# Low halves of w1 moved to ScalarE and GpSimd in the ramp, the first softmax cut in two, and one visit moved up a list

## The chip, the cores and the metric

The kernel runs on one core of a Trainium2 chip. The metric is the device time of one execution in microseconds (us); the median of three runs is compared. The engines are called as the profile calls them: PE (TensorE matmul) with PEld (its weight load), DVE (VectorE), ACT (ScalarE), POOL (GpSimd), and SP (SyncE, which here issues DMAs). Each engine executes its instructions in the order of its own queue. A DMA that is issued from SP's queue waits there for its data, and everything behind it waits too.

## The reference

Two stages follow each other, in float32:

- A causal convolution with weights of its own for each token: for 8 sequences of 2880 tokens with 192 channels, `weight_gen` gives 8 heads x 7 taps for each token. A softmax over the 7 taps (maximum subtracted, exponential, divided by the sum plus 1e-9) makes the weights, and `out[b,s,h*24:(h+1)*24] = sum over k of w[b,s,h,k] * x[b,s-6+k,h*24:(h+1)*24]`, with zeros ahead of a sequence.
- A routed mixture of experts on the 23040 results: the best of 4 groups by `x @ w_group`, then the best of its 4 experts by `x @ w_expert[g]`, so one of 16 experts for each token. The token's output is `gate * (relu(x @ w1[g,e]) @ w2[g,e])`, with w1 of 192x1024 and w2 of 1024x192. The gate is the product of the two softmax values.

## The kernel before, in words

**Tiling.** The 23040 tokens lie as 128 partitions x 180 columns, and 15 groups of 12 columns are worked through in order (`front`, line 612). A group's convolution (`conv`, 284) has two chunks of 6 columns. For each tap DVE multiplies the chunk's inputs by the weights (`product`, L289, 128x1152). In the first six chunks the products are summed on PE, by a matmul with the identity into PSUM (L330); `SUMS` says which taps DVE adds by itself beforehand (L325). The products lie in a ring of three buffers, `pr`. ACT then copies the sums out of PSUM (L333). Later chunks are added on DVE alone (L307).

**Routing.** `logits` (359) takes a chunk: ACT copies the last 64 channels aside (`rem`, L379), PE transposes the rows (L386, L387), ACT copies the transposes (L393), PE multiplies by the router's weights (L369, L410), ACT copies the logits (`ls`, L413). `ranks` (417) is a row of some 30 small DVE instructions from L341 to L480; the last one writes `posi`, the position of every token in a table `rows` in HBM that is sorted by expert. Then POOL sends the group's 12 columns there, one indirect DMA each (`scatter_row`, L494).

**Visits.** After certain groups a list is made (`table`, 508) of full blocks of 128, 256 or 384 rows of one expert; `ROUNDS` says after how many groups, and how many visits of 3, 2 and 1 blocks each list holds. A visit loads its rows (`xb`, L750, on SP) and its expert's weights, does the two matmuls (L878, L916) and scatters the result (L933, on POOL). The first list comes after two groups and holds ten visits of one block, which multiply in plain float32. In the later visits w1 and x are split into a high part, rounded to `float32r`, and a low part. What is left of w1's last 64 rows after the rounding, the low half, is made once at the start for all 16 experts by `halves` (580), two experts at a time, and stored in HBM as `w1lo`; later visits read it.

**Ramp.** The stretch up to the first visit is called the ramp here: groups 0 and 1 through convolution, routing and scattering.

**Order.** The instructions of PE, ACT, DVE and SP are issued in the order in which the Python code emits them; POOL's order is chosen by the framework's scheduler. The code is a set of generators that yield what an instruction costs by the kernel's own table, and `clk` is the planner's clock for each engine, the sum of these costs. It sets the order and measures nothing. `front` steps through `conv`; after each of its yields `beside` (622) lets side work move: `slow` (the halves), `side` (the next group's softmax), and `routing`. A generator that yields `NEXT` is not moved again until `state["unit"]` has changed, and that goes up with each finished sum of products.

**The halves before.** `next(slow[0][0])` issues the 16 loads at the start. From group 2 on (`g >= FIRST`, line 624) each call of `beside` moves one step: ACT casts a pair to its high part (L591, into one shared buffer `hi`), then DVE subtracts (L593) and SP stores two results (L595).

Of the kernel before, what the change touches and what calls it, by code (L numbers as in the profile page):

```python
# [1 line left out]

# [6 lines left out]
F32 = mybir.dt.float32  # L9
F32R = mybir.dt.float32r  # L10
# [3 lines left out]
ALU = mybir.AluOpType  # L14
# [2 lines left out]
DRAM = bass.MemoryType.DRAM  # L17

WIDTHS = (12,) * 15
ROUNDS = ((2, 0, 0, 10), (3, 0, 4, 0), (4, 0, 5, 0), (5, 0, 7, 0), (6, 0, 5, 0), (7, 0, 7, 0), (8, 0, 5, 0), (9, 0, 6, 0), (10, 0, 7, 0), (11, 0, 5, 0), (12, 1, 4, 0), (13, 0, 5, 0), (14, 0, 6, 0), (15, 10, 6, 2))  # L20
LATE = (1.0, 3.0, 3.0)
AHEAD = (1.0, 1.0, 2.5)
HURRY = 12
# [1 line left out]
WHOLE = 12  # L25
SINGLE = tuple((k,) for k in range(7))
MIXED = ((0, 1), (2,), (3,), (4,), (5,), (6,))
FOUR = ((0, 1, 2), (3, 4), (5, 6))
FIVE = ((0, 1), (2, 3), (4,), (5,), (6,))
HALF = ((0, 1), (2, 3), (4, 5), (6,))  # L30
SUMS = (MIXED, FIVE, FIVE, FIVE, FIVE, FIVE)


class Slot:
# [4 lines left out]
def conv_moe_kernel(ctx: ExitStack, tc: tile.TileContext, x, wgen, w_group, w_expert, w1, w2, out):  # L39
    nc = tc.nc  # L40
    B, SEQ, D = x.shape
    H, K = wgen.shape[2], wgen.shape[3]
    G, EG = w1.shape[0], w1.shape[1]
    F = w1.shape[3]
    P = 128
    HG = D // H
    NE = G * EG
# [4 lines left out]
    SG = 12  # L52
    SC = 6
# [11 lines left out]
    MAXB = NTOK // BK  # L65
    NR = len(ROUNDS)
    ENDS = [r[0] for r in ROUNDS]
    COL = [sum(WIDTHS[:g]) for g in range(len(WIDTHS) + 1)]
# [5 lines left out]
    FIRST = ENDS[0]  # L74
    MAIN = next(r[0] for r in ROUNDS if r[1] or r[2])
    kinds = ((3, 1), (2, 2), (1, 3))

    sure = 0
    for r in ROUNDS[:-1]:
        for nb, c in kinds:  # L80
            sure = max(sure, min(sure + nb * UB * r[c], COL[r[0]] * P - NE * (nb * UB - 1)))
    left = (NTOK - sure + NE * (BK - 1)) // BK
    TAIL = max(0, -(-(left - ROUNDS[-1][2]) // TB))

# [3 lines left out]
    pool = lambda name, bufs=1, **kw: ctx.enter_context(tc.tile_pool(name=name, bufs=bufs, **kw))  # L88
# [5 lines left out]
    wp = pool("wp")  # L94
# [14 lines left out]
    grp = {}  # L109
# [88 lines left out]
    def ring(name, n, shape, dt=F32):  # L198
        tiles = [const.tile(shape, dt, name=f"{name}{i}") for i in range(n)]
        at = [0]  # L200

        def take(i=None):
            at[0] += 1
            return tiles[(at[0] if i is None else i) % n]
        return take
# [17 lines left out]
    new_raw = [ring(f"raw{i}", m, [P, n]) for i, (n, m) in enumerate(((F, 2), (F, 2), (NFT * D, 1)))]  # L223
# [11 lines left out]
    clk = {"pe": 0.0, "act": 0.0, "dve": 3.0, "pool": 0.0}  # L235
    HOP = 0.15

    def run(eng, cost, *deps):
        clk[eng] = max([clk[eng]] + [d + HOP for d in deps]) + cost
        return clk[eng]  # L240
# [8 lines left out]
    NEXT = object()  # L249
# [3 lines left out]

    TINY = 0.2

    def softmax(g):
        wt, n = grp[g].wt, WIDTHS[g] * H
        cost = 0.08 + 0.7 * WIDTHS[g] / SG
        m = cv.tile([P, SG * H, 1], F32, name="m", bufs=1)[:, 0:n, :]
        nc.vector.tensor_reduce(out=m, in_=wt, axis=AX.X, op=ALU.max)  # L260
        yield cost
        nc.vector.tensor_tensor(out=wt, in0=wt, in1=m.broadcast_to([P, n, K]), op=ALU.subtract)
        nc.scalar.activation(out=wt, in_=wt, func=AF.Exp)
        texp = run("act", cost, clk["dve"] + cost)
        yield cost
        yield Until(texp + LATE[0])
        z = cv.tile([P, SG * H, 1], F32, name="z", bufs=1)[:, 0:n, :]
        nc.vector.tensor_reduce(out=z, in_=wt, axis=AX.X, op=ALU.add)
        yield cost
        nc.vector.tensor_scalar(out=z, in0=z, scalar1=1e-9, scalar2=None, op0=ALU.add)  # L270
        yield TINY
        nc.vector.reciprocal(out=z, in_=z)
        yield 0.08 + 0.6 * WIDTHS[g] / SG
        nc.vector.tensor_tensor(out=wt, in0=wt, in1=z.broadcast_to([P, n, K]), op=ALU.mult)
        yield cost

# [3 lines left out]
    def sum_banks(k):  # L280
        at = [(3 * k + i) % 4 for i in range(3)] if k < CHUNK[FIRST] else [2, 0, 1]
        return [banks[a]([P, 2, D]) for a in at]

    def conv(g, o):
# [3 lines left out]
        def product(c0, k, dst):  # L288
            nc.vector.tensor_tensor(  # L289
                out=dst, in0=o.xin[:, c0 + k:c0 + k + SC, :].rearrange("p s (h g) -> p s h g", g=HG),  # L290
                in1=w4[:, c0:c0 + SC, :, k:k + 1].broadcast_to([P, SC, H, HG]), op=ALU.mult)

        for n, c0 in enumerate(range(0, WIDTHS[g], SC)):
            row = o.xrow[n]
            acc = row[:, :, 0:D].rearrange("p s (h g) -> p s h g", g=HG)
            new = lambda: cv.tile([P, SC, H, HG], F32, name="pr", bufs=3)
            if state["slots"] or CHUNK[g] + n >= len(SUMS):
                product(c0, 0, acc)
# [13 lines left out]
            pieces = sum_banks(CHUNK[g] + n)  # L312
            pattern = SUMS[CHUNK[g] + n]
            for j, ks in enumerate(pattern):
# [193 lines left out]
    def table(r):  # L508
# [13 lines left out]
        yield 0.6  # L522
        todo = [(nb, c) for nb, c in ((kinds[0], kinds[2], kinds[1]) if last else kinds) if ROUNDS[r][c] or last and nb == 2]
        for nb, c in todo:
# [55 lines left out]
    def halves():  # L580
        spare = wp.tile([P, 3, F], F32, name="wa", bufs=3)
        raws = [spare[:, k, :] for k in range(3)]
        raws.append(wp.tile([P, NFT, D], F32, name="wc", bufs=4).rearrange("p f d -> p (f d)")[:, 0:F])
        raws += [new_raw[k]() for k in range(2) for _ in range(2)]
        hi = new_raw[2]()[:, 0:F].bitcast(F32R)
        for raw, e in zip(raws, range(0, NE, 2)):
            for h in range(2):
                nc.sync.dma_start(out=raw[h * HP:(h + 1) * HP, :], in_=w1v[e + h, P:D, :])
        yield NEXT
        for raw, e in zip(raws, range(0, NE, 2)):  # L590
            nc.scalar.copy(out=hi, in_=raw)  # L591
            yield Until(run("act", 0.95))
            nc.vector.tensor_tensor(out=raw.bitcast(F32R), in0=raw, in1=hi.bitcast(F32), op=ALU.subtract)  # L593
            for h in range(2):
                nc.sync.dma_start(out=w1lo[e + h], in_=raw[h * HP:(h + 1) * HP, :])  # L595
            yield 1.13

    def set_up():
        nc.gpsimd.memset(tri, 1.0)
# [8 lines left out]

    scoring, ranking = [], []
    slow = [[halves(), None]]  # L610

    def front():
        side = []
        set_up()
        load_group(1)
        next(slow[0][0])
        yield from softmax(0)

        def pace(g):
            return 99 if g <= FIRST else HURRY if g < MAIN + 3 else 8 if g in ENDS else 2  # L620

        def beside(g, n):
            rush = g >= FIRST and not grp[FIRST - 1].routed
            if g >= FIRST and not rush:
                for q in list(slow):
                    yield from move(slow, q, 1)
            for q in side[:1]:
                if not rush:
                    yield from move(side, q, 3)
            yield from routing(g)  # L630

        def routing(g):
            if ranking:
                yield from move(ranking, ranking[0], pace(g))
            if scoring and (not ranking or g < FIRST):
                yield from move(scoring, scoring[0], pace(g) if scoring[0][2].chunks == 2 or g >= FIRST - 1 else 3)

        def settle(g):
            while not grp[g].routed:
                qs = ranking or scoring  # L640
                q = qs[0]
                yield from move(qs, q, 99)
                if qs and qs[0] is q and q[1] is not None:
                    yield Until(q[1][1]) if q[1][0] == "time" else NEXT

        for g in range(ENDS[-1]):
            o = grp[g]
            o.routed = False
            scoring.append([logits(g, o), None, o])
            for n, c in enumerate(conv(g, o)):  # L650
                yield c
                if n == (2 if state["slots"] else 0) and 1 <= g < ENDS[-1] - 1:
                    load_group(g + 1)
                if n >= (12 if state["slots"] else 4) and not o.ahead and g + 1 < ENDS[-1] and g != FIRST - 1:
                    o.ahead = True
                    side.append([softmax(g + 1), None])
                yield from beside(g, n)
                if g == FIRST - 1 and n in (7, 8):
                    if n == 7:
                        soft = softmax(FIRST)  # L660
                    yield next(soft)
            if g == FIRST - 1:
                for n, c in enumerate(soft):
                    yield c
                    yield from beside(g, n)
            yield from finish_all(side)
            if g:
                yield from settle(g - 1)
        yield from settle(ENDS[-1] - 1)
# [8 lines left out]
    def move(qs, q, most):  # L678
        for _ in range(most):
# [15 lines left out]
            else:  # L695
                yield c

    fr = front()

    def step():  # L700
# [446 lines left out]
```

## Time and profile before

| | us |
|---|---|
| median of 3 runs | 1255.02 |
| lowest, highest | 1247.34, 1255.09 |
| the profiled execution | 1256.81 |
| its span | 1255.2 |
| PE, DVE, ACT, POOL busy in it | 1162.0, 968.2, 651.6, 557.4 |

The page gives busy times and a chain that ended last. For a change in the ramp the timeline says more: it lists one engine's instructions in order of time, and in brackets the idle time before one and what ended it. A busy time of small instructions in a row can overlap a little, since each is counted from its issue to its end.

### The profile page before, as it was taken

What the parts mean: (1) busy time and instruction counts of PE and PEld (TensorE: products, weight loads), DVE (VectorE), ACT (ScalarE), POOL (GpSimd) and SP (SyncE); (2) the same over time, 40 slices, a digit from 0 to 9 for tenths busy, and PEclk for the clock granted to TensorE, in tenths of its full rate; (3) what the DMA queues carried; (4) which work ended last, traced back from release to release, by engine and by line L of the source; (5) the groups of instructions that cost most, each with busy time, mean ns of one, the idle gap of its engine ahead of it and who ended that gap; (6) DMA issues with size and microseconds to landing.
All of it is one profiled execution on the core that took longest, in us unless ns stands there. A gap on an engine that the chain in (4) does not pass through costs nothing.

```text
span 1255.2 us, 24437 instructions
## 1 busy us (share of the span) xinstructions
PE 1162.0 (93%) x8357; PEld 1087.6 (87%) x8357; DVE 968.2 (77%) x1648; ACT 651.6 (52%) x1234; POOL 557.4 (44%) x598
## 2 busy tenths in 40 slices
PE   5886996979999999999999999997999989999995
PEld 2443886879999999999999999997899989999995
DVE  8897895968989999999998988886554756666560
ACT  1122443536556655566555655544556656666561
POOL 6133171635547465746573737372656212222121
PEclk9897898979999999999999999998899989999998
DMA  9228789966877887978786878637678775555661
GB/s 264 92 101 253 233 263 288 255 203 196 276 235 260 249 267 233 289 217 284 214 299 204 285 224 292 192 105 247 183 230 234 235 205 150 153 157 156 182 191 37
DMA packets 81734, 270.89 MB, mean 216 GB/s; under 512 B 15063, under 2 KB 31734, under 8 KB 79808
## 3 DMA queue, kind: packets, MB, share of 16 engines
q1 hardware_dynamic: 62424, 229.77, 60.1%
q0 software_dynamic: 19056, 39.20, 9.5%
q8 instruction: 67, 1.10, 0.4%
q14 instruction: 67, 0.55, 0.2%
q10 hardware_dynamic: 120, 0.28, 0.1%
HBM read 225.83 MB, written 44.23 MB: 215 GB/s over the span
## 4 chain that ended last, share of the span: by engine, by line
PE 56%; issue 20%; DMA 7%; POOL 7%; DVE 6%; ACT 2%; SPq 1%; POOLq 0%; ACTq 0%; DVEq 0%
PE py L916 24%; PE ph L878 23%; POOL out L933 4%; DVE pr L289 2%; POOL rows L494 2%; DMA xb<-rows 2%; PE pl L369 2%; PE tp L386 1%; DMA raw<-in_moe_w 1%; DMA raw<-w1lo 1%; PE tpx L853 1%; PE tpx L852 1%; DMA wa<-in_moe_w 1%; PE ph L330 1%; PE tp L387 1%
## 5 line engine op out<-in xcount | busy, mean ns | idle before, releaser
L878 PE MATMUL ph<-xh,wa 128*128 128x256 f32 (+1 forms) x1992 | 468.2, 309 | 0.0
L933 POOL DMA_INDIRECT out<-y,xb x189 | 212.9, 1126 | 485.6 <-ACT y L925 215.0
L916 PE MATMUL py<-wc,hh 128*128 128x192 f32 x2160 | 404.1, 329 | 5.6 <-ACT y L925 5.6
L878 PE MATMUL ph<-xl,wa 128*128 128x256 f32 (+1 forms) x1328 | 360.5, 290 | 0.0
L916 PEld LDWEIGHTS py<-wc,hh 128*128 128x128 f32 x2160 | 349.6, 192 | 5.8 <-ACT y L925 5.8
L878 PEld LDWEIGHTS ph<-xh,wa 128*128 128x128 f32 x1992 | 338.9, 191 | 7.0 <-issue 5.6
L884 ACT ACTIVATE hh<-ph 128x512 f32<-128x512 f32 (+2 forms) x296 | 165.6, 560 | 271.2 <-PE ph L878 271.2
L878 PEld LDWEIGHTS ph<-xl,wa 128*128 128x128 f32 x1328 | 252.1, 190 | 0.0
L289 DVE TENSOR_TENSOR pr<-xin,wt 128x1152 f32<-128x1152 f32 x186 | 248.8, 1350 | 4.0 <-PE py L330 1.9
L494 POOL DMA_INDIRECT rows<-xrow,ix x156 | 215.3, 1380 | 52.3 <-POOL ix L493 33.0
L307 DVE TENSOR_TENSOR xrow<-xrow,pr 128x1152 f32<-128x1152 f32 x144 | 194.7, 1352 | 0.6
L811 DVE SCALAR_TENSOR_TENSOR pr<-ph,hh 128x384 fp32r<-128x384 f32 (+1 forms) x128 | 77.5, 605 | 105.0 <-ACT hh L889 103.8
L811 DVE TENSOR_TENSOR wa<-raw,wa 128x1024 fp32r<-128x1024 f32 x83 | 101.3, 1220 | 40.2 <-ACT wa L787 40.2
L918 PE MATMUL py<-wc,hh 128*128 128x384 f32 x352 | 112.8, 367 | 0.0
L493 POOL COPY ix<-posi 128x1 int32<-128x1 int32 x156 | 70.7, 463 | 80.5 <-DMA rows<-xrow,ix 44.6
L889 ACT ACTIVATE hh<-ph 128x384 fp32r<-128x384 f32 (+1 forms) x128 | 68.6, 536 | 69.6 <-PE ph L878 69.5
L787 ACT CAST wa<-raw 128x1024 fp32r<-128x1024 f32 x83 | 87.1, 1049 | 7.6 <-DMA raw<-in_moe_w 7.6
L919 PE MATMUL py<-wc,pr 128*128 128x192 f32 x352 | 89.0, 253 | 0.0
L796 ACT CAST wa<-raw 128x1024 fp32r<-128x1024 f32 x83 | 86.8, 1046 | 1.1 <-DMA raw<-w1lo 1.1
L811 DVE TENSOR_TENSOR xl<-tpx,xh 128x512 fp32r<-128x512 f32 (+1 forms) x94 | 61.6, 655 | 28.3 <-ACT xh L858 27.1
L925 ACT ACTIVATE y<-py,xb 128x192 f32<-128x192 f32 x179 | 67.4, 424 | 23.1 <-PE py L916 21.6
L393 ACT COPY xT<-tp 128x384 f32<-128x384 f32 x84 | 40.4, 481 | 62.4 <-PE pl L369 33.6
(172 smaller groups left out, 1392.5 us busy)
## 6 DMA issues: line engine op xcount, KB each, us to landing
wc<-in_moe_w SPq DMA_DIRECT2D x73, 768.0 KB, 5.5
raw<-in_moe_w SPq DMA_DIRECT2D x83, 512.0 KB, 5.2
xin<-in_x SPq DMA_DIRECT2D x14, 1728.0 KB, 10.0
raw<-in_moe_w SPq DMA_DIRECT2D x91, 256.0 KB, 5.0
raw<-w1lo SPq DMA_DIRECT2D x83, 256.0 KB, 6.5
raw<-in_moe_w SPq DMA_DIRECT2D x22, 768.0 KB, 7.8
xb<-rows SPq DMA_DIRECT2D x72, 194.0 KB, 4.4
wa<-in_moe_w SPq DMA_DIRECT2D x24, 384.0 KB, 5.8
```

The lines of the kernel that those rows point to most:

```text
L289: nc.vector.tensor_tensor(out=dst, in0=o.xin[:, c0 + k:c0 + k + SC, :].rearrange("p s (h g) -> p s h g", g=HG), in1=w4[:, c0:c0 + SC, :, k ...
L307: nc.vector.tensor_tensor(out=acc, in0=acc, in1=prs[k - 2], op=ALU.add)
L494: written_once(nc.gpsimd.indirect_dma_start(out=rows[:, :], out_offset=bass.IndirectOffsetOnAxis(ap=ix, axis=0), in_=src, in_offset=None, ...
L787: nc.scalar.copy(out=o.wa[:, 0, :], in_=o.raw[0])
L796: nc.scalar.copy(out=o.wa[:, 2, :], in_=o.raw[1])
L811: f(*a, **k)
L878: nc.tensor.matmul(ph[:, v, :], lhsT=w[:, f0:f0 + P], rhs=rhs, start=i == 0, stop=i == len(terms) - 1)
L884: nc.scalar.activation(out=hh, in_=ph, func=AF.Relu)
L916: nc.tensor.matmul(b.acc[t], lhsT=hh[:, v, c], rhs=wc[0][:, f, :], start=f == 0 and not (b.wide and t == 1), stop=f == NFT - 1 and not (b. ...
L918: nc.tensor.matmul(b.py[t], lhsT=hh[:, v, c], rhs=wc[f // 4][:, f % 4].rearrange("p l d -> p (l d)"), start=f == 0, stop=False)
L919: nc.tensor.matmul(b.acc[t], lhsT=hl[:, v, c], rhs=wc[f // 4][:, f % 4, 0, :], start=False, stop=f == NFT - 1)
L933: ins = nc.gpsimd.indirect_dma_start(out=out[:, :], out_offset=bass.IndirectOffsetOnAxis(ap=b.x.bitcast(I32)[:, t, D + 1:D + 2], axis=0), ...
```

## The change

Four edits.

1. `halves` no longer uses DVE. ACT casts a pair into one of two buffers in turn (`his`, in a tile of the ring `wa`), POOL subtracts, SP stores, all emitted in one step. The steps start when the planner's clock of DVE is past 44, in whatever group, where they started with group 2.
2. The first group's softmax is done for its first six columns ahead of the convolution. The six instructions for the other six columns are emitted one after each of the first six yields of the convolution.
3. The first chunk takes its taps from the last to the first, and the two that DVE adds are 6 and 5 (before: 0 and 1).
4. The tenth list holds six visits of two blocks instead of five, the eleventh three instead of four.

```diff
-ROUNDS = (... (11, 0, 5, 0), (12, 1, 4, 0), ...)
+ROUNDS = (... (11, 0, 6, 0), (12, 1, 3, 0), ...)
...
+TURNED = ((6, 5), (4,), (3,), (2,), (1,), (0,))
-SUMS = (MIXED, FIVE, FIVE, FIVE, FIVE, FIVE)
+SUMS = (TURNED, FIVE, FIVE, FIVE, FIVE, FIVE)
...
-    def softmax(g):
-        wt, n = grp[g].wt, WIDTHS[g] * H
-        cost = 0.08 + 0.7 * WIDTHS[g] / SG
+    def softmax(g, a=0, b=None):
+        b = b or WIDTHS[g]
+        wt, n = grp[g].wt[:, a * H:b * H, :], (b - a) * H
+        cost = 0.08 + 0.7 * (b - a) / SG
...
-        hi = new_raw[2]()[:, 0:F].bitcast(F32R)
+        other = wp.tile([P, 3, F], F32, name="wa", bufs=3)
+        his = [other[:, k, :].bitcast(F32R) for k in range(2)]
...
-        for raw, e in zip(raws, range(0, NE, 2)):
+        for k, raw in enumerate(raws):
+            e, hi = 2 * k, his[k % 2]
             nc.scalar.copy(out=hi, in_=raw)
-            yield Until(run("act", 0.95))
-            nc.vector.tensor_tensor(out=raw.bitcast(F32R), in0=raw, in1=hi.bitcast(F32), op=ALU.subtract)
+            nc.gpsimd.tensor_tensor(out=raw, in0=raw, in1=hi.bitcast(F32), op=ALU.subtract)
+            run("pool", 2.0, run("act", 1.0))
             for h in range(2):
                 nc.sync.dma_start(out=w1lo[e + h], in_=raw[h * HP:(h + 1) * HP, :])
-            yield 1.13
+            yield NEXT
...
-        yield from softmax(0)
+        yield from softmax(0, 0, SC)
+        rest = softmax(0, SC)
...
-            if g >= FIRST and not rush:
+            if clk["dve"] > 44 and not rush:
                 for q in list(slow):
                     yield from move(slow, q, 1)
...
                 yield c
+                if g == 0 and n < 6:
+                    for c in islice(rest, None if n == 5 else 1):
+                        yield c
```

## Rows read from the trace of the kernel before

**Rows 1.** The page's slices: PE's busy tenths in 40 slices of the span.
```profile
PE   5886996979999999999999999997999989999995
```

**Rows 2.** Timeline: end of the ramp; start, duration, engine, line, operation, tiles.
```profile
99.93 13.95 SPq L595 DMA_DIRECT2D w1lo<-wa  x6
...
107.69 0.97 POOL L494 DMA_INDIRECT rows<-xrow,posi  x1 [0.30 <-issue]
...
115.57 1.97 SPq L750 DMA_DIRECT2D xb<-rows  x2
...
117.63 0.63 PE L843 MATMUL tp<-ident,xb 128*96 128x128 f32 x2 [3.76 <-DMA xb<-rows]
```

**Rows 3.** Tile view of `rows`: how long its DMAs took to land.
```profile
DMA to landing us min/median/max: 2.4/5.0/9.0
```

**Rows 4.** Timeline: the first softmax and the first chunk.
```profile
4.38 1.28 ACT L263 ACT_TABLE_LOAD   x1 [4.38 <-DMA wt<-in_weight_gen]
...
6.60 0.85 DVE L268 TENSOR_REDUCE z<-wt 128x96 f32<-128x672 f32 x1 [0.83 <-ACT wt L263]
...
9.51 2.65 DVE L289 TENSOR_TENSOR pr<-xin,wt 128x1152 f32<-128x1152 f32 x2
...
13.69 1.62 PE L330 MATMUL ph<-pr,ident 128*128 128x384 f32 x2 [13.69 <-POOL first L161]
```

**Rows 5.** Timeline: group 0's logits and ranks.
```profile
46.68 0.36 ACT L413 COPY ls<-pl 128x240 f32<-128x240 f32 x1 [0.64 <-PE pl L410]
...
48.35 0.49 DVE L426 TENSOR_TENSOR sel<-ls,ohg 128x192 f32<-128x192 f32 x1
...
49.73 0.21 DVE L349 SCALAR_TENSOR_TENSOR dfe<-de,j 128x48 f32<-128x48 f32 x1
...
55.74 0.17 DVE L480 SCALAR_TENSOR_TENSOR posi<-pos 128x12 int32<-128x12 f32 x1
```

**Rows 6.** Timeline: the first and the last of group 0's twelve scatters on POOL.
```profile
56.80 2.09 POOL L494 DMA_INDIRECT rows<-xrow,posi  x1 [34.96 <-DVE wt L262]
...
74.12 0.97 POOL L494 DMA_INDIRECT rows<-xrow,posi  x1 [0.30 <-issue]
```

**Rows 7.** Timeline: group 1, from its first chunk's logits to its ranks.
```profile
64.31 0.51 ACT L379 COPY rem<-xrow 128x384 f32<-128x384 f32 x1
...
66.82 0.91 PE L330 MATMUL py<-pr,ident 128*128 128x384 f32 x2
...
69.06 3.90 DVE L289 TENSOR_TENSOR pr<-xin,wt 128x1152 f32<-128x1152 f32 x3 [0.52 <-PE ph L330]
...
83.75 0.19 DVE L341 TENSOR_REDUCE mxg<-ls 128x12 f32<-128x48 f32 x1
```

**Rows 8.** Timeline: POOL beside DVE, at the start and later.
```profile
3.85 0.73 POOL L159 TENSOR_SCALAR first<-sgn 128x16 f32<-128x16 f32 x3
...
9.79 3.86 POOL L161 TENSOR_SCALAR first<-first 128x16 f32<-128x16 f32 x3
...
230.30 2.74 DVE L307 TENSOR_TENSOR xrow<-xrow,pr 128x1152 f32<-128x1152 f32 x2
...
231.72 1.37 POOL L493 COPY ix<-posi 128x1 int32<-128x1 int32 x1 [4.75 <-DMA rows<-xrow,ix]
```

**Rows 9.** Timeline: POOL's largest elementwise instruction, and one cast of the halves on ACT.
```profile
0.91 1.06 POOL L119 MEMSET xin<- 128x1152 f32 x1 [0.29 <-POOLq L1130]
...
101.89 1.05 ACT L591 CAST raw<-wa 128x1024 fp32r<-128x1024 f32 x1
```

**Rows 10.** Timeline: after the first visit's start, up to the idle time behind list one.
```profile
122.18 1.23 DVE L593 TENSOR_TENSOR wc<-wc,raw 128x1024 fp32r<-128x1024 f32 x1 [6.90 <-ACT raw L591]
...
136.33 0.36 ACT L413 COPY ls<-pl 128x240 f32<-128x240 f32 x1 [0.99 <-PE pl L410]
...
140.53 0.19 DVE L341 TENSOR_REDUCE mxg<-ls 128x12 f32<-128x48 f32 x1
...
209.44 1.65 PE L916 MATMUL py<-wc,hh 128*128 128x192 f32 x4 [5.60 <-ACT y L925]
```

More of the change, by code (lines that the diff above doesn't have):

```diff
@@ L1 @@
 from contextlib import ExitStack
+from itertools import islice
 import concourse.bass as bass
@@ L19 @@
 WIDTHS = (12,) * 15
-ROUNDS = ((2, 0, 0, 10), (3, 0, 4, 0), (4, 0, 5, 0), (5, 0, 7, 0), (6, 0, 5, 0), (7, 0, 7, 0), (8, 0, 5, 0), (9, 0, 6, 0), (10, 0, 7, 0), (11, 0, 5, 0), (12, 1, 4, 0), (13, 0, 5, 0), (14, 0, 6, 0), (15, 10, 6, 2))
+ROUNDS = ((2, 0, 0, 10), (3, 0, 4, 0), (4, 0, 5, 0), (5, 0, 7, 0), (6, 0, 5, 0), (7, 0, 7, 0), (8, 0, 5, 0), (9, 0, 6, 0), (10, 0, 7, 0), (11, 0, 6, 0), (12, 1, 3, 0), (13, 0, 5, 0), (14, 0, 6, 0), (15, 10, 6, 2))
 LATE = (1.0, 3.0, 3.0)
@@ L272, in softmax @@
         nc.vector.reciprocal(out=z, in_=z)
-        yield 0.08 + 0.6 * WIDTHS[g] / SG
+        yield 0.08 + 0.6 * (b - a) / SG
         nc.vector.tensor_tensor(out=wt, in0=wt, in1=z.broadcast_to([P, n, K]), op=ALU.mult)
```

## The prediction

> **What bounds the kernel now.** I read the page's slices first. From the tenth slice (282 us) on, PE stands at nine tenths or more in nearly all of them [rows 1], so a microsecond won or lost before that is mostly kept to the end. The low digits lie in the first nine slices, and all that the change moves lies there too, but for one visit. So the ramp is read next, as a timeline. It ends with the first visit's transposes at 117.63, released by its rows [rows 2]. Group 1's last scatter left POOL at 108.66. The load of the rows was issued only at 115.57, because SP stood at the stores of the halves for 13.95 us, waiting for DVE's subtractions. Two things therefore bound the ramp: the path convolution, logits, ranks, scatter of groups 0 and 1, and behind it SP's queue. After the first visit the next loss that a list explains is PE's 5.60 us ahead of 209.44 [rows 10].
>
> **Edit 2 and 3, the first softmax and the taps.** The sums of its first six columns start once ACT's table is loaded (5.66, rows 4) and an exponential of half the length is done: the 0.94 us up to 6.60 become some 0.5. From there to the first product are 2.9 us of DVE, half of that now. The first product starts near 7.7, 1.8 us sooner. The other six columns cost DVE half of 4.6 us (the 2.9, and two instructions like the 0.85 us reduction) and a little for more starts: 2.4 us, placed among the first products. PE's first sum needs two products and an addition and now has two of these pieces among them (0.9 us): it starts 0.9 us sooner than 13.69. At the end of the chunk the balance is between -0.9 (PE carries it through) and +0.6 (2.4 less 1.8). I take 0, in the middle. Taps from the last let the first product do without the six columns that come from the neighbour; in the rows DVE waits for no such load, so this alone is priced at 0, and its cover is that the loads landed before 9.51.
>
> **Edit 1, where the pairs stand.** The order follows from the code. The planner's clock passes 44 after the first addition of group 1's first chunk (44.9 when its costs are summed; this is an order, not a time). One pair is emitted for each new unit: pair 1 there, pair 2 after the next tap, pair 3 just ahead of group 0's ranks. Then come the ranks and POOL's twelve scatters. Pairs 4 and 5 follow behind them, pair 6 behind ACT's copies of that chunk's sums and **ahead of `rem`**, pairs 7 and 8 in the next chunk. Casts alternate between two buffers, so the cast of pair 6 waits until POOL has subtracted pair 4.
>
> *Price of a subtraction on POOL.* No row shows one. DVE takes 1.23 us for it [rows 10]. POOL's largest elementwise row, a fill of 1152 columns, takes 1.06 [rows 9], so 0.94 for 1024. The subtraction reads two tensors: at one pass 0.94, at two 1.9, at three (two reads, a write) 2.8. I take 1.9, one pass for each input. The Trainium skill ("GPSIMD Engine Reference", section "3.1 Elementwise") gives 4497 ns for such an instruction of 2048 columns, by which I estimate 2.25 us here, and the sum would be 1.4 us higher; no run here shows it yet.
>
> *DVE and POOL.* Three small POOL instructions take 0.73 us together at 3.85, beside a reduction, and 3.86 us at 9.79, beside products that read two tensors: 1.29 each, a product's length [rows 8]. At 231.72 a copy of one column lasts 1.37 us under two additions, and these last 2.74 where two products of the same size take 2.65 [rows 4, 8]. So POOL waits for such a DVE instruction to end, and DVE, as far as a tiny copy can show it, waits for POOL in turn. I take it that a subtraction on POOL stops DVE's two-tensor instructions for its length. The Trainium skill ("SBUF — State Buffer", section "SBUF: two separate sides") states this as a lock on the ports that the two share, held for the whole instruction by whoever came first. By that rule the cost below stands; without it the forecast is the rival "side by side". It speaks against this edit, and the trace agrees on POOL's side.
>
> *Group 0's ranks.* ACT is free after `ls` (47.04), the first cast ends at 48.1, and the first subtraction starts near 48.3, when DVE comes to the instruction at 48.35 [rows 5]. DVE gets one two-tensor instruction in after each subtraction: 48.3 + 1.9, then 0.5, then 1.9, then 0.2, then 1.9, is 54.7 for the instruction that stood at 49.73: **+5.0**. Ends: 0 without the exclusion, +7.7 at 2.8 us each.
>
> *The wait ahead of `rem`.* `posi` then ends at 60.9 instead of 55.91, and the twelve scatters, back to back from 56.80 to 75.09 [rows 6], end at 80.1. Only then comes pair 4's subtraction (0.3 us between POOL's instructions, 1.9) until 82.3, pair 6's cast (1.05 and a hop of 0.1) until 83.45, and `rem`, which stood at 64.31 [rows 7]: **+19.1**. Queued behind that cast on ACT are `rem` and the copies of the transposes; PE waits for these with the next chunk's sums (66.82) behind them, and DVE stops when the three product buffers are full. The excess over the 5.0 is the new wait, 14.1 us. Ends: 0 (pair 4 goes ahead of the scatters), or 14.1 less or more 0.9, by the price of the subtraction.
>
> *From there to group 1's `posi`.* Subtractions 5 and 6 fall into DVE's stop. 7 and 8 may stop DVE among the last products (0 to 3.8 us); DVE has run ahead into the products that stood at 69.06, which gives some back. I set both at 0. So group 1's ranks, at 83.75 before, and its scatters are 19.1 late.
>
> *SP and DVE at the ramp's end.* The stores now wait for POOL, and are done with pair 8, well before group 1's scatters end. Behind them in SP's queue stands only group 3's load, needed 20 us later. A scatter takes 2.4 to 5.0 us to land [rows 3], so the rows can be loaded 2.4 to 5.0 after the last one leaves POOL, where it was 6.9: 1.9 to 4.5 less. I take **-3.2**, the middle. The low end is 0: DVE loses three subtractions there, and the planner, which books none of them, puts as many products ahead of the first visit.
>
> *After the first visit.* DVE no longer subtracts, nor waits for ACT's cast (6.90 us ahead of one at 122.18). Group 2's logits were copied at 136.69, and DVE came to them at 140.53, 3.8 us later; one more subtraction of 1.2 lies between that and the list. **-5.0**, if the list is that much sooner and the 5.60 us of PE shrink with it [rows 10]. Ends: 0 and -5.6.
>
> **Edit 4.** The tenth and eleventh list hold 12 visits together before and after, and PE's slices there (22 to 27 of 40) are all 9; the 7 behind them lies at the twelfth list [rows 1]. No wait stands at the head of the eleventh: 0.
>
> **Sum.** 0 + 5.0 + 14.1 - 3.2 - 5.0 = +10.9. The profiled execution (1256.8) would become 1267.7. It lies 1.8 above the median of the runs (1255.0), so I forecast a median of **1265.9**, 0.9% slower.
>
> **The rivals.**
> - *No wait ahead of `rem`* (faster): POOL's order is the scheduler's. If it sends pair 4 ahead of the scatters, and the engines run side by side, the ramp's path is as before, and -3.2 and -5.0 remain: 1246.8. Decided by whether the fourth subtraction has ended by 62, when `rem` could start. For it: POOL idles up to 56.80. Against it: the twelve scatters are ready together and were emitted first, and nothing came between them before [rows 6].
> - *Side by side* (POOL's subtractions don't stop DVE, but the wait stands): 14.1 - 8.2 = +5.9, 1260.9. For it: DVE's loss under POOL is shown for a tiny copy only.
> - *Exclusion without the wait*: eight subtractions of 1.9 are 15.2 us of DVE in the ramp, less the 0.5 it idled there [rows 7], less 8.2: +6.5, 1261.5.
>
> **How the numbers follow.** The forecast has a chance of 0.50, no wait 0.22, side by side 0.15, exclusion alone 0.08; 0.05 is left for what I don't see. The forecast's own range is 1258 (cheap subtractions, both credits whole) to 1275 (2.8 us each, half of the credits). To hold 8 in 10 the range takes in "no wait" at 1246.8: 1246 to 1275. A measurement of this kernel tells about 1% (12.6 us) from no change. The forecast lies 1.7 us within that bound, so some two fifths of it count as slower, and most of the two middle rivals as the same; "no wait" reaches -12.6 only if both credits are at their ends and the first softmax gains too. Slower 0.30, same 0.61, faster 0.09.
>
> **What would show it.** Right: in the new trace ACT idles between the copies at L333 of group 1's first chunk and `rem`, released by POOL; the fourth subtraction starts behind twelve scatters; `rem` is at 80 to 86; group 0's `posi` is near 61; the load of the first rows follows the last scatter by less than 5 us; PE's gap near 209 is smaller. Wrong: subtractions 4 to 8 end before 70, `rem` near 64, DVE's products of usual spacing beside POOL's subtractions, or a POOL subtraction outside 0.9 to 2.8 us.

## The result, and the profile after

| | kernel before | changed kernel |
|---|---|---|
| first comparison, 12 runs each: median us | 1250.79 | 1257.26 |
| ratio, 95% interval | | 1.0056 [1.0038, 1.0074] |
| second comparison, another chip: median us | 1258.22 | 1269.38 |
| ratio, 95% interval | | 1.0093 [1.0057, 1.0128] |
| profiled execution (first comparison), span | 1256.81, 1255.2 | 1261.24, 1259.6 |

The changed kernel is slower, by 0.4 to 1.3%. The forecast was 1265.9, 0.9% (10.9 us) slower. The first comparison's difference of 6.5 us lies 4 us under that, the second's of 11.2 on it. The first median itself lies 8.6 us under 1265.9; 4.2 of these come from the kernel before, whose median was 1255.02 in the three runs that the forecast started from and is 1250.79 in twelve. The ramp went much as forecast; two later terms were wrong by some 10 us or more each, and they have opposite signs.

The page's slices of the changed kernel, PE's busy tenths and the granted clock in 40 slices of 31 us (before: [rows 1]):

```profile
PE   5657898899999999999999999969999989999995
PEclk9877899899999999999999999979999989999998
```

Of the first five slices three are lower and one is higher, the sixth to ninth are together a little higher, and the 7 at the 28th slice has become a 6 at the 27th: a stall far from the ramp has moved and grown.

The timeline of the changed kernel, several engines in order of time (line numbers are 3 to 9 higher than before; to be read beside [rows 4], [rows 5], [rows 6], [rows 7] and [rows 2]):

```profile
7.85 1.36 DVE L292 TENSOR_TENSOR pr<-xin,wt 128x1152 f32<-128x1152 f32 x1
...
47.63 0.36 ACT L416 COPY ls<-pl 128x240 f32<-128x240 f32 x1 [0.64 <-PE pl L413]
...
49.02 7.08 POOL L597 TENSOR_TENSOR wa<-wa 128x1024 f32<-128x1024 f32 x3 [27.35 <-ACT wa L596]
49.06 2.37 DVE L358 TENSOR_TENSOR ohg<-dfg,ixg 128x48 f32<-128x48 f32 x1
51.46 2.47 DVE L429 TENSOR_TENSOR sel<-ls,ohg 128x192 f32<-128x192 f32 x1
...
62.20 0.17 DVE L483 SCALAR_TENSOR_TENSOR posi<-pos 128x12 int32<-128x12 f32 x1
62.67 1.44 POOL L497 DMA_INDIRECT rows<-xrow,posi  x1 [6.58 <-DVE posi L483]
...
78.72 0.98 POOL L497 DMA_INDIRECT rows<-xrow,posi  x1 [0.30 <-issue]
79.70 2.37 POOL L597 TENSOR_TENSOR wc<-wc,wa 128x1024 f32<-128x1024 f32 x1
82.11 1.05 ACT L596 CAST wa<-raw 128x1024 fp32r<-128x1024 f32 x1 [12.99 <-POOL wc L597]
83.06 0.51 ACT L382 COPY rem<-xrow 128x384 f32<-128x384 f32 x1
88.17 5.79 POOL L597 TENSOR_TENSOR raw<-raw,wa 128x1024 f32<-128x1024 f32 x2 [1.48 <-ACT wa L596]
88.95 6.22 DVE L292 TENSOR_TENSOR pr<-xin,wt 128x1152 f32<-128x1152 f32 x2 [13.96 <-PE ph L333]
...
113.80 0.17 DVE L483 SCALAR_TENSOR_TENSOR posi<-pos 128x12 int32<-128x12 f32 x1
...
130.02 0.98 POOL L497 DMA_INDIRECT rows<-xrow,posi  x1 [0.30 <-issue]
132.66 1.47 SPq L759 DMA_DIRECT2D xb<-rows  x2
...
217.25 1.65 PE L925 MATMUL py<-wc,hh 128*128 128x192 f32 x4 [3.19 <-ACT y L934]
```

Two lines of the kernel before stand against these:

```profile
48.11 0.21 DVE L355 TENSOR_TENSOR ohg<-dfg,ixg 128x48 f32<-128x48 f32 x1
...
91.58 0.17 DVE L480 SCALAR_TENSOR_TENSOR posi<-pos 128x12 int32<-128x12 f32 x1
```

Read from the top: a comparison of 48 columns (`ohg`) that DVE did in 0.21 us before lasts 2.37 beside POOL's first subtraction. The fourth subtraction stands behind the twelfth scatter, ACT waits 12.99 us for it, and `rem` follows at 83.06 (64.31 in [rows 7]; forecast 83.45). Group 1's `posi` is at 113.80; it was at 91.58. The rows' load is 1.7 us behind the last scatter's end; it was 6.9 behind [rows 2].

What was not foreseen lies later. The line in which PE waits longest for rows, with what came ahead of it, in the changed kernel:

```profile
824.84 0.98 POOL L497 DMA_INDIRECT rows<-xrow,ix  x1 [0.28 <-POOL ix L496]
826.12 0.97 POOL L942 DMA_INDIRECT out<-y,xb  x1 [0.30 <-issue]
827.40 0.97 POOL L942 DMA_INDIRECT out<-y,xb  x1 [0.30 <-issue]
828.61 0.34 SPq L759 DMA_DIRECT2D xb<-rows  x1
831.46 0.48 PE L861 MATMUL tpx<-ident,xb 128*128 128x128 f32 x1 [11.06 <-DMA xb<-rows]
```

And in the kernel before:

```profile
848.71 0.97 POOL L933 DMA_INDIRECT out<-y,xb  x1 [0.30 <-issue]
...
851.25 0.34 SPq L750 DMA_DIRECT2D xb<-rows  x1
853.79 0.47 PE L852 MATMUL tpx<-ident,xb 128*128 128x128 f32 x1 [7.63 <-DMA xb<-rows]
```

In both, the load of rows that PE waits for follows *result* scatters (`out<-y,xb`) that stood behind a group's row scatters on POOL. That it waits for them is tried below. The windows of the changed kernel behind that stall (stretch, length, busy us by engine with counts, granted clock, DMA share, GB/s) show what it costs beyond itself:

```profile
831.40:836.00 4.60, 4.48 (x16) 4.19 (x17) 2.95 (x3) 3.73 (x8) 0.45 (x1) 0.50 0.98 325
836.00:841.00 5.00, 5.00 (x34) 4.98 (x34) 2.71 (x4) 2.74 (x6) 2.05 (x2) 0.81 1.02 321
```

PE had been idle for 11.06 us. A granted clock of 0.50 is the level of 1.2 GHz: 4.48 x 0.50 + 5.00 x 0.19 = 3.2 us more by this estimate, so that the stall costs about 14 us. In the kernel before the two stretches behind the 7.63 us (853.7 to 858.3 and on to 863.3) have 0.50 and 0.83, so the old stall cost some 3 us beyond itself as well.

The gap between the two profiles, in us: group 1's `posi` +22.2 (113.80 - 91.58); the rows' load +17.1 (132.66 - 115.57); the 16th result of a visit +2.7 (279.48 - 276.83, fences below); the wait for rows +3.4 (11.06 - 7.63); the span +4.4. The 1.7 us by which 2.7 and 3.4 exceed 4.4 were not followed. So in these two profiles 14.4 us of the ramp's loss were given back by 280 us, where 5.0 were forecast, and 3.4 were lost where 0 was forecast. Three more profiles of kernels whose order is the changed kernel's up to there, set against the same profile of before, give back 18.5 (the changed kernel once more), 19.8 (no shared block) and 7.6 (edit 4 undone): the size is known to several us only, but each is more than the 5.6 that the prediction set as its limit.

### The profile page after: what moved, and what is told of

The parts are those of the page before. It is cut to its first block, busy times and chain, and to the rows that moved or that the text cites. A ratio compares the mean times of both kernels' runs of the same rounds, so it can differ in the third digit from the quotient of the medians.

```text
span 1259.6 us, 24444 instructions
## 1 busy us (share of the span) xinstructions
PE 1157.3 (92%) x8357; PEld 1086.2 (86%) x8357; DVE 969.3 (77%) x1646; ACT 652.4 (52%) x1235; POOL 578.6 (46%) x606
## 4 chain that ended last, share of the span: by engine, by line
PE 58%; issue 21%; POOL 8%; DMA 6%; DVE 2%; ACT 2%; SPq 1%; POOLq 0%; ACTq 0%; DVEq 0%
PE py L925 25%; PE ph L887 25%; POOL out L942 3%; POOL rows L497 2%; PE pl L372 2%; DMA raw<-w1lo 2%; PE tp L389 1%; DMA raw<-in_moe_w 1%; DMA xb<-rows 1%; PE tpx L862 1%; PE tpx L861 1%; DMA out<-y,xb 1%; PE tp L390 1%; DVE pr L292 1%; ACT xT L396 1%
## 5 line engine op out<-in xcount | busy, mean ns | idle before, releaser
L292 DVE TENSOR_TENSOR pr<-xin,wt 128x1152 f32<-128x1152 f32 x186 | 252.7, 1370 | 17.5 <-PE ph L333 14.0
L497 POOL DMA_INDIRECT rows<-xrow,ix x156 | 219.4, 1406 | 50.4 <-POOL ix L496 35.2
L496 POOL COPY ix<-posi 128x1 int32<-128x1 int32 x156 | 68.1, 447 | 68.2 <-DMA rows<-xrow,ix 34.0
L820 DVE TENSOR_TENSOR xl<-tpx,xh 128x512 fp32r<-128x512 f32 x94 | 61.7, 656 | 24.8 <-ACT xh L867 24.1
```

The costliest lines, as they stand in the source:

```text
L292: nc.vector.tensor_tensor(out=dst, in0=o.xin[:, c0 + k:c0 + k + SC, :].rearrange("p s (h g) -> p s h g", g=HG), in1=w4[:, c0:c0 + SC, :, k ...
L497: written_once(nc.gpsimd.indirect_dma_start(out=rows[:, :], out_offset=bass.IndirectOffsetOnAxis(ap=ix, axis=0), in_=src, in_offset=None, ...
L820: f(*a, **k)
```

## The experiments

Two theories were tried for each surprise. *The ramp*: the wait ahead of `rem` is the price, or the lock of DVE by POOL is. *What was given back*: DVE's time (its subtractions have left the stretch after the first visit), or the order in which the planner writes the instructions there. *The late stall*: a buffer shared by visits, or the scatters and lists themselves. Each run is compared with the kernel before on its own chip.

**Edit 4 undone** (the changed kernel with the old lists).
```
-ROUNDS = (... (11, 0, 6, 0), (12, 1, 3, 0), ...)
+ROUNDS = (... (11, 0, 5, 0), (12, 1, 4, 0), ...)
```


> The changed kernel with the lists of the kernel before (edit 4 undone). Theory: the only visit of three blocks, first of the eleventh list, takes three of the four block places of its buffer, so its rows can be loaded only when the visit three places ahead of it has written its results, and these stand on POOL behind twelve scatters; the moved visit puts this wait at 11.1 us where the order of before had 7.6 us. Undone, PE's longest wait for rows after 800 us is 7 to 8 us, and the time is 3 us below the changed kernel's, ratio to the kernel before about 1.003. Rival: the larger wait comes from the convolution standing 8 us further ahead there; then it stays near 11 us and the ratio at 1.0056.


Measured: 1254.9, ratio 0.9953 [0.9928, 0.9979]. PE waits 0.2 us in all for rows between 780 and 880. The direction was the theory's, the size not: not 3 us but about 13 (1.0056 less 0.9953, of 1257) hang on the moved visit, or 18 by the second comparison's 1.0093; the three ratios come from different chips. With the old lists PE's stall is not 7.6 but gone. Edits 1 to 3 alone make the kernel *faster* than before.

**Edit 4 alone** (the kernel before with the new lists).


> The kernel before with edit 4 alone. Theory: the moved visit puts the visit of three blocks at the buffer whose last user writes its results behind group 12's scatters, whatever the convolution's lead; PE waits there for its rows at visit 62 for 10 us or more, where before it waited 7.6 us at visit 64; 3 to 10 us longer, ratio 1.003 to 1.008. Rival, the moved visit hurts only together with the earlier convolution of the changed kernel: the wait at visit 62 stays under 8 us, ratio 0.997 to 1.001.


Measured: 1251.92, ratio 0.9961 [0.9931, 0.9991]. The wait at the moved place is small:
```profile
862.81 0.33 PE L852 MATMUL tpx<-ident,xb 128*128 128x128 f32 x1 [2.15 <-DMA xb<-rows]
```
The theory fails: the new lists don't hurt by themselves, they even save most of the old stall. They hurt only together with the changed kernel's order. POOL's order in the traces shows how the two meet. Visits are counted from 0, and a visit has as many results as blocks. Visit 62, the first of the eleventh list, is the one of three blocks; its load follows the results of visit 59. With edit 4 alone 110 results, those of visits 0 to 59, stand on POOL ahead of the thirteenth group's row scatters, and visit 62's rows are loaded before these start:
```profile
814.34 0.34 SPq L750 DMA_DIRECT2D xb<-rows  x1
815.84 0.98 POOL L494 DMA_INDIRECT rows<-xrow,ix  x1 [0.16 <-POOL ix L493]
```
In the changed kernel only 108 stand ahead, and the two of visit 59 come behind the twelve row scatters, at 826.12 and 827.40.

**No shared block** (the changed kernel with one wider buffer). A buffer of rows has four blocks. Visits use three buffers in turn. Visits of two blocks take a buffer's halves in turn, the only visit of three blocks in the middle of the program takes the first three blocks. So it shares a block with the visits three places ahead of it and behind it. The wider buffer ends that:
```
-xbs = [const.tile([P, 4, W], ...) for i in range(3)]
-h = 0 if nb == 3 else n // 3 % 2 * 2
+xbs = [const.tile([P, 5 if i == 2 else 4, W], ...) for i in range(3)]
+h = 0 if nb == 3 else n // 3 % 2 * (3 if n % 3 == 2 else 2)
```


> The changed kernel with one of the three buffers of rows five blocks wide instead of four, so that the visit of three blocks shares no block with the visits three places ahead of it and behind it; the order of every engine is unchanged. Theory: its load no longer waits for the results that stand behind group 12's scatters, PE's 11.1 us at 831 fall below 3, ratio 0.995 to 0.998 (9 to 11 us below the changed kernel). Rival: the load waits for those scatters themselves or for its list, the 11 us stay, ratio as the changed kernel's.


Measured beside the changed kernel itself on one chip: 1253.71 against 1269.38, ratios 0.9973 [0.9945, 1.0002] and 1.0093 [1.0057, 1.0128]. The load that was issued at 828.61 is issued at 800.48, and PE's wait is gone:
```profile
800.48 0.34 SPq L759 DMA_DIRECT2D xb<-rows  x1
```
The order of instructions on ACT, DVE, POOL and in SP's queue is the same in both traces, so the 15.7 us (11 of stall, the clock behind it, and 1 or 2 within the spread of the runs) are the shared block's.

**The same in the kernel before** (`i == 1`, `n % 3 == 1`: there the visit of three blocks is number 61, in the second buffer).


> The kernel before with the buffer that its visit of three blocks uses made five blocks wide, so that this visit shares no block with its neighbours; the order of every engine is unchanged. Theory of the shared buffer: PE's 7.6 us at 853.8 fall below 3 and the time by 4 to 7 us, ratio 0.994 to 0.997. Rival, that wait is the list's or the scatters' own: unchanged, 0.999 to 1.001.


Measured: 1243.94 against 1251.94, ratio 0.9922 [0.9905, 0.994], better than the theory's range; PE no longer waits there. The kernel before had the same fault at another place: its three-block visit, 61, was the one that the visit three places later, 64, waited for (the load at 851.25 is the 65th; the three result scatters ahead of it are visit 61's).

**The changed kernel once more.**


> The changed kernel itself once more, beside the experiments of this call. Every theory: ratio near the 1.0056 found first; a ratio of 0.999 or less would say that the comparisons made on different chips can't be set side by side.


Measured: 1269.38, ratio 1.0093 [1.0057, 1.0128], PE's wait 11.57. The two intervals overlap.

**Five buffers for the high parts** (the changed kernel; no cast waits for a subtraction behind the scatters).
```
+his = ... (five buffers)
...
-e, hi = 2 * k, his[k % 2]
+e, hi = 2 * k, his[(0, 1, 0, 1, 2, 3, 4, 0)[k]]
```


> The changed kernel with five buffers for the high parts instead of two, so that no cast waits for a subtraction that stands behind the scatters; order and engines unchanged. Theory of the wait: rem, at 83.1 in the changed kernel, comes back to about 71 (64.3 and the 6.5 by which group 0's ranks are late); POOL still subtracts pairs 4 to 8 in one row behind the scatters, 11.8 us from 80 on, and DVE loses at most half of that; group 1's posi at 100 to 107 instead of 113.8; the time 6 to 12 us below the changed kernel's, ratio 0.996 to 1.001. Rival, the lock is the price: the five subtractions stop DVE in its products, group 1's posi stays at 110 or later, ratio 1.003 to 1.006.


Measured: 1268.25, ratio 1.0083 [1.0045, 1.0121]. Its timeline:
```profile
70.81 0.51 ACT L382 COPY rem<-xrow 128x384 f32<-128x384 f32 x1
...
81.36 2.38 POOL L599 TENSOR_TENSOR wc<-wc,wa 128x1024 f32<-128x1024 f32 x1
81.44 11.58 DVE L273 TENSOR_SCALAR z<-z 128x96 f32<-128x96 f32 x1
83.67 2.37 POOL L599 TENSOR_TENSOR raw<-raw,wa 128x1024 f32<-128x1024 f32 x1
...
90.61 2.33 POOL L599 TENSOR_TENSOR raw<-raw,wa 128x1024 f32<-128x1024 f32 x1
...
110.50 0.17 DVE L483 SCALAR_TENSOR_TENSOR posi<-pos 128x12 int32<-128x12 f32 x1
```
The wait is gone (`rem` 12.3 us sooner) and hardly anything is won: group 1's `posi` comes 3.3 us sooner. DVE stands for 11.58 us in an instruction of 96 columns, through all five subtractions. The lock is the price, as the rival said (1.0083 is even above the rival's 1.003 to 1.006); in the changed kernel the wait only covered it.

**The subtractions on DVE, at the new place** (the changed kernel; five buffers, each subtraction three steps behind its cast).
```
-nc.gpsimd.tensor_tensor(out=raw, ...)
...
+raw, e = raws[k - 3], 2 * (k - 3)
+nc.vector.tensor_tensor(out=raw.bitcast(F32R), ...)
```


> The changed kernel with the subtractions on DVE, three steps behind the casts and with five buffers, so that all eight fall between the ranks of group 0 and of group 1; everything else as changed. Theory: no lock and no wait; eight subtractions of 1.23 us lie on DVE's path in the ramp, group 1's posi at 101 to 103 (91.6 before, 113.8 changed), the load of the first rows near 121; what the changed kernel gave back after the first visit (some 13 us by 290 us) comes from DVE having no subtractions there and is kept: ratio 0.994 to 0.998. Rival: what was given back came only from the visits starting late, so that stalls further on had gone by then; with visits 5 us late about 5 us is given back and the wider visit still costs 3: ratio 1.001 to 1.004.


Measured: 1255.85, ratio 0.997 [0.9941, 0.9998]:
```profile
99.37 0.17 DVE L483 SCALAR_TENSOR_TENSOR posi<-pos 128x12 int32<-128x12 f32 x1
...
119.27 1.46 SPq L763 DMA_DIRECT2D xb<-rows  x2
...
827.31 0.48 PE L865 MATMUL tpx<-ident,xb 128*128 128x128 f32 x1 [11.84 <-DMA xb<-rows]
```
Group 1's `posi` is 14.4 us sooner than with POOL. The visits start 13.4 us sooner and keep that (16th result 265.89, changed 279.48): what was given back does not shrink when the visits start early. The rival falls. The 11.8 us stall is there as well.

**The place alone** (the kernel before, halves as in the last run, no other edit).


> The kernel before with one thing changed: the halves begin where the changed kernel begins them, with five buffers for the high parts and the subtractions on DVE three steps behind the casts (no edit 2, 3 or 4). Theory: group 0's posi near 56.5, group 1's near 98.5, 12 to 13 us given back by 300 us as in the run with the subtractions on DVE, and the wait of 7.6 us at the twelfth list gone as in the run with the lists put back: ratio 0.985 to 0.992. Rival: the wait at the twelfth list stays, ratio 0.993 to 0.997.


Measured: 1241.75, ratio 0.9879 [0.9841, 0.9918]; `posi` of group 1 at 98.63; PE doesn't wait for rows between 780 and 880. This version beats both kernels. It doesn't show what the place is worth by itself: its new code books nothing for a subtraction either, so it has the changed kernel's order too, and the order alone reaches 0.9905, with an interval that overlaps this one (last run below).

**Edits 2 and 3 alone.**


> The kernel before with edits 2 and 3 alone (first softmax for six columns, taps from the last). Theory: the first product starts 1.7 us sooner and the extra instructions on DVE cost 2.6, so group 0's first logits are copied about 0.95 us later than before (47.6 instead of 46.7) and the time is 0 to 1 us longer, ratio 1.000 to 1.001. Rival: the 0.95 us come from the loads of the halves or from another edit, and the logits are copied at 46 or earlier.


Measured: 1261.26, ratio 1.0002 [0.9975, 1.0029]. The first product is at 7.88, the first logits are copied at 47.37. The changed kernel's 47.63 had looked 0.95 late against 46.68 [rows 5], but among these runs kernels *without* the two edits copy theirs at 46.63 to 47.83: no cost is shown, and no gain.

**The changed kernel without its subtractions.**
```
-nc.gpsimd.tensor_tensor(out=raw, in0=raw, in1=hi.bitcast(F32), op=ALU.subtract)
```


> The changed kernel without its eight subtractions on POOL (the stored low halves are then the unsplit rows of w1); casts, stores, lists and the order of all else stay. Theory: the whole lateness of group 1's posi (113.8 against 91.6) is POOL's subtractions, by lock and by wait; without them rem is near 66 and posi near 93 to 95, and at the first rows' load near 112 to 114. The convolution is then 20 us further ahead of where the changed kernel has it, so the wait of 11 us at visit 62 may move: ratio 0.980 to 0.990. Rival, casts and stores carry part of it: posi at 98 or later, ratio above 0.990.


Measured: 1239.31, ratio 0.9889 [0.9873, 0.9906]:
```profile
91.27 0.17 DVE L483 SCALAR_TENSOR_TENSOR posi<-pos 128x12 int32<-128x12 f32 x1
...
111.30 1.51 SPq L758 DMA_DIRECT2D xb<-rows  x2
...
809.97 0.48 PE L860 MATMUL tpx<-ident,xb 128*128 128x128 f32 x1 [11.14 <-DMA xb<-rows]
```
Group 1's `posi` is where it was before (91.58): all 22 us are POOL's subtractions, and casts and stores cost nothing there. And with everything 20 us sooner the stall keeps its 11 us: it hangs on the order, not on the times.

**The kernel before without its subtractions.**


> The kernel before without its eight subtractions on DVE (the stored low halves are then the unsplit rows of w1); casts, stores and the order of all else stay. Theory: what the changed kernel gave back after the first visit is what DVE's subtractions, with their waits for the casts, cost at the old place; without them the rows' load is issued near 111 instead of 115.6, and of the stalls near 209 and 264 (5.6 and 4.8 us) most is gone: 12 to 17 us less by 300 us, ratio 0.985 to 0.991. Rival, the give-back comes from the other order of casts and products: only the 4 us at the rows' load and the 5 us of the forecast, ratio 0.993 to 0.997.


Measured: 1243.27, ratio 0.993 [0.9907, 0.9952], at the edge of the rival's range. The 4 us that both theories put at the rows' load are not there. Stores, load and the 16th result in this run:
```profile
99.12 7.72 SPq L594 DMA_DIRECT2D w1lo<-wa  x6
...
114.84 1.49 SPq L749 DMA_DIRECT2D xb<-rows  x2
...
271.00 0.75 ACT L924 ACTIVATE y<-py,xb 128x192 f32<-128x192 f32 x2 [0.78 <-PE py L915]
```
The stores leave SP's queue at 106.84 instead of 113.88 (99.93 + 13.95, [rows 2]), and the load comes only 0.7 us sooner: something else would have held it as long in the kernel before, the scatters' landing as far as the trace tells. The 16th result is 5.8 us sooner than in the profile of before (276.83). Two more kernels with the order of before up to there, edit 4 alone and the wider buffer, have it at 275.24 and 276.42, so DVE's time is worth 4 to 6 us.

**One number of the planner** (the kernel before; work, engines and place unchanged).
```
-            yield 1.13
+            yield 0.0
```


> The kernel before with one number changed: the planner books 0.0 instead of 1.13 for a subtraction of the halves; the work, its engines and its place in the ramp stay, only the order written behind the first visit differs (group 3's logits are copied after the results of 5 visits instead of 7). Theory of the order: what the changed kernel gave back after the first visit comes from this order; group 3's posi at 203 to 208 instead of 222.4, the stalls near 209 and 264 (5.6 and 4.8 us) small or gone, the wait of 7.6 us at the twelfth list gone as in the run with early halves and the old lists: 10 to 17 us in all, ratio 0.986 to 0.992. Rival, the give-back is DVE's time: its subtractions still stand there, ratio 0.997 to 1.001.


Measured: 1238.24 against 1251.1, ratio 0.9905 [0.9877, 0.9933]. How many results of visits ACT has copied when group 3's logits are copied, first the kernel before (up to 194.6 us; line, engine, operation, count, duration in ns, first and last start):
```profile
L925 ACT ACTIVATE y<-py,xb x7: 421/421/422, 144.5 to 188.0; 128x192 f32<-128x192 f32 x7
```
The changed kernel (up to 198.5):
```profile
L934 ACT ACTIVATE y<-py,xb x5: 420/420/421, 158.1 to 187.7; 128x192 f32<-128x192 f32 x5
```
This run (up to 183.7):
```profile
L925 ACT ACTIVATE y<-py,xb x5: 421/421/422, 143.8 to 174.7; 128x192 f32<-128x192 f32 x5
```
And the 16th result, in the kernel before, the changed kernel, and this run:
```profile
276.83 0.75 ACT L925 ACTIVATE y<-py,xb 128x192 f32<-128x192 f32 x2 [1.02 <-PE py L916]
```
```profile
279.48 0.75 ACT L934 ACTIVATE y<-py,xb 128x192 f32<-128x192 f32 x2 [0.27 <-PE py L925]
```
```profile
266.41 0.75 ACT L925 ACTIVATE y<-py,xb 128x192 f32<-128x192 f32 x2 [0.28 <-PE py L916]
```
10.4 us are won against this profile of before, 8.8 against the earliest of the three with its order, though group 1's `posi` (92.43) and the rows' load (118.52) are no sooner and DVE still subtracts at the old place. The planner no longer books the halves after the first visit, so it writes group 3's convolution two visits sooner: its `posi` is at 200.04 (222.44 before, 213.56 in the changed kernel), and its list is there in time. The stall near 209 stayed (5.96), against the expectation; the one near 264 is gone. In the kernel before that was:
```profile
264.54 0.47 PE L387 MATMUL tp<-ident,rem 128*128 128x128 f32 x1 [4.76 <-ACT rem L379]
```

**The late stall, put together** (PE's wait for rows in us, between 780 and 880; the order is counted by the results copied ahead of group 3's logits; the runs with 7 have visit 59's results on POOL ahead of the thirteenth group's row scatters, those with 5 behind them):

| | old lists | new lists |
|---|---|---|
| order of 7 results | before 7.63, e5 6.03, n2 7.41 | edit 4 alone 2.15 |
| order of 5 results | e1 0.2; e7, o1 none | after 11.06, again 11.57, e3 11.54, e4 11.84, n1 11.14 |
| no shared block | b1 none (order of 7) | e6 none (order of 5) |

(e1 is edit 4 undone, e3 five buffers, e4 DVE at the new place, e5 edits 2 and 3 alone, e6 and b1 the wider buffer, e7 the place alone, n1 and n2 without subtractions, o1 the planner's number.)

## Why the prediction was right or wrong

- **First softmax and taps, 0**: right within what can be told (1.0002). The first product at 7.85 was forecast at 7.7.
- **Group 0's ranks, +5.0**: +6.5 (62.20 - 55.74, [rows 5]). The mechanism is right, the price was low: a subtraction takes 2.31 us by the starts of the five in a row (81.36 to 90.61), not 1.9. Of the 6.5, 0.95 are the logits that came later (47.63), which runs without these edits show too; the ranks themselves lost 5.5. The estimate of 2.25 that the prediction drew from the Trainium skill ("GPSIMD Engine Reference", section "3.1 Elementwise") was nearer, and the trace agrees with it within 3%.
- **The lock**: shown, by the 2.37 us comparison, by the 11.58 us beside five subtractions, and by `posi` at 91.27 without them; "side by side" is refuted. The Trainium skill ("SBUF — State Buffer", section "SBUF: two separate sides") gives the same rule, a port pair held for the whole instruction; the trace agrees.
- **The wait ahead of `rem`, +14.1**: the place, the releaser and the time (83.06) were right, the worth was not. Taking the wait away (five buffers) wins 3.3 us of `posi`, and nothing that the time shows. The subtractions that "fall into DVE's stop" lock DVE as soon as there is no stop, all five of them (11.58 us); 14.1 and the lock are two names for the same time. The rival "exclusion without the wait" put this at 14.7 for all eight; the run with five buffers has 18.9 (110.50 - 91.58).
- **Group 1's `posi`, +19.1**: +22.2. `rem` was 18.8 late, as forecast within 0.4; the other 3.4 came behind it, with subtractions 7 and 8, which lock DVE's products at 88.95 (6.22 us for two, where two take 2.65 in [rows 4]) and had been set at 0, with an end of 3.8.
- **SP, -3.2**: -5.1. The load is issued 2.6 us behind the last scatter's start (130.02) and 1.7 behind its end: the 2.4 to 5.0 us of [rows 3] count from a scatter's issue, not from when it leaves POOL, and that is one of the two us. The reason given, SP's stores, is not enough: without DVE's subtractions the stores leave SP 7 us sooner, and the load comes only 0.7 us sooner (n2).
- **After the first visit, -5.0: the first step that failed.** It took one idle row [rows 10] for all that could be won and set the low end at -5.6. It was -14.4 (7.6 to 19.8 by other profiles). Alone, the order brings the 16th result 9 to 10 us forward, and DVE's time 4 to 6; whether the two add up was not tried. The prediction noted that the planner books none of the moved subtractions, and drew only a loss ahead of the first visit from it.
- **Edit 4, 0: the second.** The two lists hold 10 visits, not 12, and the 7 in the 28th slice is not at the twelfth list, as the prediction and later expectations have it: the wait at 853.79 is visit 64's, the fourth of the eleventh list (visits 61 to 65), a list that edit 4 changes. So the term was read off the wrong list. "No wait stands at the head of the eleventh" was true of the kernel before, and no bound for the kernel after. The visit of three blocks shares a block with the visits three places to either side. Which of them has its results behind a group's scatters on POOL follows from lists and order together, and both were changed. With the old lists the stall of 7.6 us and the 3 of clock behind it would have gone (e1); instead an 11 us stall and 3 us of clock came.

So the likeliest mechanism was right for the ramp, 15.9 forecast against 17.1 at the rows' load. Behind it the edits but the fourth bring the kernel to 0.9953 of before, about -6, so that some 23 us (17.1 + 6, the old stall's among them) are won there instead of 5; and the moved visit costs 13 to 18 instead of 0. The sum came out as near to the forecast as it did because these two errors nearly cancel, and that is luck.

## What to carry to other kernels

When work leaves an engine in a kernel whose order is written by a planner, ask first what the planner will write differently: one booked number was worth 1% here (0.9905), at least as much as leaving out the work it stood for (0.993). A buffer that is shared between a few odd-sized items is a wait that any change of order can wake; look for its users on every queue, and not only for waits that the trace shows now. Elementwise work handed from DVE to POOL was paid by DVE again here, nearly twice over (2.31 us of lock for 1.23 us of work).

## What the runs showed of the hardware that was not expected

- Between two POOL subtractions in a row DVE sometimes got one instruction in (the comparison ends at 51.43, between the first and the second) and sometimes none (11.58 us through five). What decides is open.
- In the run with the subtractions on DVE, ACT stands still for 3.03 us near 441 to 444 with no engine's work as releaser. PE waits 2.25 us for its copy, and the granted clock of the next 5 us is 0.66. Other runs show such pauses at other times. The runs of one kernel spread by 3 to 17 us; whether these pauses are the cause was not tried.
